# A pre-LN linear-attention and GeGLU block on one core: the opening loads reordered over two rings, two tiles only centred, and the rest of the layernorm taken in pairs

## The chip, the cores and the metric

The kernel runs on one core of a Trainium2 chip. The metric is device time in microseconds (us) of one execution; lower is better. Before the change the median of 16 runs is 194.26 us (193.64 to 194.85).

## The reference

x is 2048 tokens of 448 features in bf16. The block is an attention without softmax, with 16 heads of 28, and a gated feed-forward part of width 1792. Each is preceded by a layernorm without weights and followed by a residual.

```python
n   = layernorm(x)                      # mean and variance over the 448 features
q, k, v = heads(n @ wqkv)               # wqkv: 448 x 1344
pq, pk  = phi(q), phi(k)                # phi(t) = (t + 1 if t > 0 else exp(t)) + 1e-6
kv  = einsum("bhsd,bhse->bhde", pk, v); z = pk summed over the tokens
h   = x + ((pq @ kv) / (pq . z + 1e-6)) @ wo
m   = layernorm(h)
out = h + (gelu(m @ w_gate) * (m @ w_up)) @ w_down
```

kv and z are sums over all the tokens, so the attention's output cannot begin before the K part of every token is done.

## The kernel before

The tokens are 16 tiles of 128. Everything stays in SBUF. The stages, by what TensorE (PE) does:

1. **Loads and warm-up.** SyncE (SP) issues x tile 0, the Q and K weights (`dwqk`, the first 384 rows, and `dwqk_t`, the 64-row tail), then x tiles 2 to 15, the V weights and wo; ScalarE (ACT) issues x tile 1 (lines 303 to 313, all through `dma`, line 284). Meanwhile PE runs 40 matmuls of 128 columns on a tile of ones (L342), whose result is not used.
2. **Layernorm 1 and projections** (`ln_tile`, `k_tile`, `q_tile`). Statistics are made on VectorE (DVE): `bnst` (L348) and `bnag` (L349). rstd is exp(-0.5 ln(var + eps)), two ACT instructions per tile: `ln` (L355), `rstd` (L357). Tiles 0 to 3 are normalized on DVE (`normD`, L370), transposed by PE in two halves (`tr0`, `tr1`, L378) and copied from PSUM by ACT (`evxA`, L383) and DVE (`evxD`, L385). Tiles 4 to 15 are normalized on GpSimd (POOL; `negm` L352, `normP` L388) and transposed by DMA from SP's queue (`xT`, L390). `k_t` and `q_t` are four accumulating matmuls each (L404). The first two read the half that ACT copied, the last two the half that DVE copied, and the fourth the weight tail. For K: `ek` (ACT exp, L415), `ck` (DVE, L416), `pk` (DVE, from PSUM, L417), then `pt_t`, four matmuls that add the normalized tile against pk (L423). For Q: `eq` and `rq` (ACT exp and relu, L431, L432).
3. **kv and w2** (L462, L471): the small matrices that join v, the heads and wo.
4. **Attention output and layernorm 2** (`a2_pair`), by pairs of tiles: `cq`, `aq` (DVE), `t1` (POOL), `dr`, `rd`, `pn` (DVE), a transpose (`tro` on PE for the first pair, `oT` by DMA for the others, L510), `out2` (PE, L523), `hr` (DVE residual), layernorm 2, and a transpose into hnT (`trh` on PE for tiles 0 and 1; `nhP` on POOL, `wrap` on DVE, `hT` by DMA, L561, for the others). w_down is loaded by one DMA, `dwd`, 1568 KB, from SP's queue.
5. **Feed-forward** by chunks of 2, 2, 4, 4, 4 tiles: `gu` (PE, L603 and L605), `ge` (ACT gelu, L623), `hm` (DVE product, L625), `down` (PE, L575), `fo` (DVE residual), `do` (output DMA).

No engine chooses its order at run time. Every piece of work is a task, numbered in the order in which the source adds it, with semaphores for its data. The five strings of `ORDERS` list the numbers of the tasks of PE, ACT, DVE, POOL and SP in the order in which that engine runs them; a waiting task holds up all that is behind it on its engine.

Of the kernel before, what the change touches and what calls it, by code (L numbers as in the profile page):

```python
# [5 lines left out]
BF16 = mybir.dt.bfloat16  # L6
F32 = mybir.dt.float32
ALU = mybir.AluOpType
# [7 lines left out]
    "26 32 34 43 63 41 66 71 76 52 59 50 61 79 84 70 87 75 99 83 116 111 91 126 103 138 115 150 162 130 174 142 154"  # L16
    " 187 200 213 219 166 229 178 191 245 204 235 217 233 179 249 192 205 218 234 250 254 251 291 257 295 299 293"
    " 260 315 297 266 319 317 263 320 269 278 275 356 333 337 272 434 439 387 444 449 454 459 418 464 506 511 516"
    " 469 526 521 490 472 531 536 578 583 588 562 541 544 593 598 603 608 613 618 623 628 633 638 643 675 648 651"
    " 706 654 657 722 727 732 737 742 747 752 757 762 767 772 777 782 787 804 809 814 819 824 829 795 792 801 798"  # L20
    " 834 839 844 849 854 859 864 869 874 877 880 883 886",
    "3 25 29 30 38 39 33 42 64 47 56 48 57 65 67 72 94 51 95 78 60 106 107 80 77 121 122 86 133 88 85 134 145 146"
    " 100 157 169 158 170 112 118 182 183 195 196 127 139 117 208 209 240 224 241 151 163 225 175 188 201 214 220"
    " 221 230 246 236 237 285 308 288 289 256 253 255 252 312 258 347 351 259 294 316 298 268 318 267 261 265 264"
    " 379 383 262 327 328 270 280 329 330 279 277 271 334 276 273 274 339 435 437 442 414 440 410 445 447 452 450"
    " 457 455 462 460 467 465 482 509 507 486 514 519 512 517 527 529 558 554 524 522 532 534 539 537 579 581 671"
    " 586 584 589 667 591 702 596 594 599 601 606 604 698 611 609 614 616 621 619 626 624 629 631 634 636 641 639"
    " 644 646 723 725 728 730 733 735 740 738 745 743 748 750 755 753 760 758 763 765 770 768 773 775 780 778 785"
    " 783 790 788 807 805 812 810 817 815 822 820 825 827 832 830 837 835 842 840 845 847 852 850 857 855 860 862"
    " 867 865 870 872",  # L30
    "27 28 36 37 31 40 35 44 45 54 46 55 92 49 93 58 104 68 105 73 53 69 62 119 74 120 131 81 132 143 82 144 89 167"
    " 155 90 156 168 101 180 206 102 181 193 113 194 114 222 207 238 128 239 223 129 140 141 340 152 153 164 165 303"
    " 176 341 177 342 304 189 301 190 202 215 302 343 216 203 231 232 372 247 248 373 374 375 286 305 287 307 290"
    " 309 311 310 346 292 350 296 300 352 313 348 314 353 349 321 382 322 378 323 324 405 325 380 331 326 381 332"
    " 335 384 336 385 406 338 357 360 358 403 359 404 361 413 362 438 409 436 443 415 411 441 412 416 475 446 448"
    " 476 367 391 453 451 388 370 392 458 477 547 456 693 463 478 481 461 389 393 390 422 468 466 548 549 485 510"
    " 508 423 487 483 488 484 419 520 518 424 515 550 401 420 513 662 421 398 660 557 528 553 691 429 523 530 555"
    " 663 432 525 694 661 559 470 560 494 491 533 535 556 540 538 692 580 582 670 495 587 473 585 666 590 566 701"
    " 668 496 567 592 563 672 669 564 492 673 565 703 493 704 545 568 597 595 600 602 697 607 605 542 612 610 699"
    " 700 615 617 622 620 627 625 630 632 635 637 640 501 676 647 645 679 504 677 576 649 680 573 681 652 678 710"  # L40
    " 711 642 707 655 708 709 658 712 724 726 729 731 720 717 734 736 741 739 689 746 744 686 749 751 756 754 761"
    " 759 764 766 771 769 774 776 781 779 786 784 791 789 808 806 813 811 818 816 823 821 826 828 833 831 796 793"
    " 799 802 838 836 843 841 846 848 853 851 858 856 861 863 866 868 873 871 875 878 881 884 887",
    "15 13 0 14 1 19 20 21 17 18 16 96 22 97 108 109 123 124 24 135 147 136 148 23 159 171 160 172 184 185 197 198"
    " 242 226 210 211 227 243 306 344 345 376 377 408 407 364 363 365 366 479 369 480 551 395 394 396 397 400 552"
    " 426 425 427 428 431 664 665 696 695 498 497 499 500 569 570 571 575 503 572 682 683 684 685 688 714 713 715"
    " 716 719",
    "2 4 5 6 7 8 9 10 11 12 98 110 125 137 149 161 173 186 199 212 228 244 281 282 283 284 354 386 417 368 371 355"
    " 489 402 399 430 433 471 561 674 474 705 546 502 577 505 574 543 656 721 718 650 653 659 690 687 797 794 803"
    " 800 879 876 885 882 888",  # L50
# [120 lines left out]
def bass_sequential_preLN__linear_attn_block__glu_gated_geglu__prompt_kernel(  # L171
# [11 lines left out]
    N_PE_TR = 4  # L183
    B1_CHUNKS = [2, 2, 4, 4, 4]
    WARM = 40
    T1_DVE = (0,)
    SEQ = "Q0 K0 K1 Q1 K2 Q2 K3 K4 K5 Q3 K6 K7 K8 K9 K10 K11 K12 K13 Q4 K14 Q5 K15 Q6 Q7 Q8 Q9 Q10 Q11 Q12 Q13 Q14 Q15"
# [3 lines left out]
    with es:  # L191
# [6 lines left out]
        xnn = sb("xnn", [128, XN_R, 512], BF16)  # L198
        xnT = sb("xnT", [128, T, 4, 128], BF16)
# [17 lines left out]
        rs1 = sb("rs1", [128, T], F32)  # L217
        st2 = sb("st2", [128, T, 6], F32)
# [29 lines left out]
        b_x = bufs("x", T)  # L248
        b_xn = bufs("xn", XN_R)
        b_xnT = [bufs("xnT%d_" % t, 2) for t in range(T)]  # L250
        b_ones2 = _Buf("ones2")
        b_wqk, b_wv = bufs("wqk", 2), bufs("wv", 2)
# [3 lines left out]
        b_epsd = _Buf("epsd")  # L256
# [34 lines left out]
        def dma_w3(q, dst, c0, c1, b, name):  # L291
            return dma(q, dst[:, 0:3, :], A_wqkv[0:384, c0:c1].rearrange("(k p) n -> p k n", p=128), [b[0]], name)
# [8 lines left out]
        for dst, b, nm_ in ((wqk_sb, b_wqk, "wqkpad"), (wv_sb, b_wv, "wvpad")):  # L301
            op("pool", lambda e, dst=dst: e.memset(dst[:, 3, :], 0.0), [], [b[1]], nm_)
        dma_x("sp", 0, 1)
        tx1 = dma_x("act", 1, 2)
        dma_w3("sp", wqk_sb, 0, 2 * D, b_wqk, "dwqk")
        dma_w1("sp", wqk_sb, 0, 2 * D, b_wqk, "dwqk_t")
        dma_x("sp", 2, 4)
        dma_x("sp", 4, 8)
# [4 lines left out]
        two = dma("sp", wo_sb[:, :, :], A_wo.rearrange("(g p) n -> p g n", p=GW), [b_wo], "dwo")  # L313
# [13 lines left out]
           [b_mtmp], [b_mask], "mask_b")  # L327
        op("pool", lambda e: e.memset(pt_sb[:, 3, :], 0.0), [], [b_pt[3]], "ptpad")
        op("pool", lambda e: e.memset(pqn[:, :, :, :, GW:128], 0.0), [], [b for l in b_pqn for b in l], "pqnpad")

        tbl1 = G.add("act", lambda e: e.preload_act_table_set("natural_log_exp_and_others"), name="tbl1", kind="nosync", after=[tx1])
# [7 lines left out]
        def warm_fn(e):  # L339
            ins = None  # L340
            for _ in range(WARM):
                ins = e.matmul(ps[:, 3, 0:128], ones_bf[:], ones_bf[:], start=True, stop=True)  # L342
            return ins
        G.add("pe", warm_fn, r=[b_ones], w=[b_ps[3]], name="warm")
# [20 lines left out]
        def ln_tile(t):  # L365
            ln_stats(t, x_sb[:, t, :], b_x[t], st1, mv1, b_st1, b_mv1, "1")
            ln_rstd_act(t, t + 1, mv1, ln1, rs1, b_mv1, b_ln1, b_rs1, "1")
            i = t % XN_R
            if t < N_PE_TR:
                op("dve", lambda e: e.tensor_scalar(xnn[:, i, 0:D], x_sb[:, t, :], mv1[:, t, 0:1], rs1[:, t:t + 1], ALU.subtract, ALU.mult),  # L370
                   [b_x[t], b_mv1[t], b_rs1[t]], [b_xn[i]], "normD_%d" % t)
                for h, (eng, k0, k1) in enumerate((("act", 0, 2), ("dve", 2, 4))):
                    bk = BK_TR[t % 2][h]

                    def ftr(e, k0=k0, k1=k1, bk=bk):
                        ins = None
                        for k in range(k0, k1):
                            ins = e.transpose(psb[:, bk, (k - k0) * 128:(k - k0 + 1) * 128], xnn[:, i, k * 128:(k + 1) * 128], ident[:])  # L378
                        return ins
                    G.add("pe", ftr, r=[b_xn[i], b_ones2, b_ident], w=[b_ps[bk]], name="tr%d_%d" % (h, t))  # L380
# [5 lines left out]
            else:  # L386
                ln_negm(t, t + 1, mv1, nm1, b_mv1, b_nm1, "1")
                op("pool", lambda e: e.tensor_scalar(xnn[:, i, 0:D], x_sb[:, t, :], nm1[:, t:t + 1], rs1[:, t:t + 1], ALU.add, ALU.mult),  # L388
                   [b_x[t], b_nm1[t], b_rs1[t]], [b_xn[i]], "normP_%d" % t)
                G.add("sp", lambda e: e.dma_start_transpose(xnT[:, t, :, :], xnn[:, i, :]), r=[b_xn[i], b_ones2], w=b_xnT[t], name="xT_%d" % t, kind="dma", after=[two])  # L390
# [16 lines left out]
        def proj_reads(t):  # L407
            return [(b_xnT[t][0], 0), (b_xnT[t][1], 2), (b_wqk[0], 0), (b_wqk[1], 3)]
# [19 lines left out]
        def q_tile(t):  # L428
            bk = slot()
            G.add("pe", lambda e, W: proj(e, W, t, bk, 0), r=proj_reads(t), w=[b_ps[bk]], name="q_%d" % t, mw=True)  # L430
            act_exp(lambda e: e.activation(eq[:, t, :], ps[:, bk, 0:D], AF.Exp), [b_ps[bk]], [b_eq[t]], "eq_%d" % t)  # L431
            act_exp(lambda e: e.activation(pq[:, t, :], ps[:, bk, 0:D], AF.Relu), [b_ps[bk]], [b_pq[t]], "rq_%d" % t)  # L432
# [258 lines left out]
```

## Time and profile before

| what | value |
|---|---|
| median of 16 runs | 194.26 us |
| the profiled execution: its time / its span | 194.31 us / 192.5 us |
| TensorE clock granted in the span | 1.0 of full speed |
| PE's stretch from the first transpose to the last matmul | 5.37 to 190.1 us |
| one projection, `pt` or `out` matmul of 448 columns, back to back | 0.189 us, four in 0.756 us |
| DVE busy from 12.02 to 18.24 us / from 50.11 to 73.42 us | 6.22 of 6.22 / 22.16 of 23.31 us |

The page gives the busy time of each engine; the timeline lists instructions in order of time; the view of waits says what an engine waited for. PE loads weights (PEld) ahead of the matmuls that use them, and matmuls overlap, so a stall may appear as a wait of PEld while PE still counts as busy. The gap between starts in the timeline, against 0.189 us for a matmul of 448 columns, is then the measure.

### The profile page before, as it was taken

What the parts mean: (1) busy time and instruction counts of PE and PEld (TensorE: products, weight loads), DVE (VectorE), ACT (ScalarE), POOL (GpSimd) and SP (SyncE); (2) the same over time, 40 slices, a digit from 0 to 9 for tenths busy, and PEclk for the clock granted to TensorE, in tenths of its full rate; (3) what the DMA queues carried; (4) which work ended last, traced back from release to release, by engine and by line L of the source; (5) the groups of instructions that cost most, each with busy time, mean ns of one, the idle gap of its engine ahead of it and who ended that gap; (6) DMA issues with size and microseconds to landing.
All of it is one profiled execution on the core that took longest, in us unless ns stands there. A gap on an engine that the chain in (4) does not pass through costs nothing.

```text
span 192.5 us, 4152 instructions
## 1 busy us (share of the span) xinstructions
PE 187.3 (97%) x1572; PEld 108.2 (56%) x1572; DVE 131.6 (68%) x355; ACT 77.9 (40%) x226; POOL 50.8 (26%) x92
## 2 busy tenths in 40 slices
PE   7989999999999899999999999999999999999994
PEld 7544455554778677564445655545556655445454
DVE  2899988999999988979957446736544442244412
ACT  3697736599954242043044420024444430044200
POOL 7068620560263387404190000450000000000000
PEclk9999999999999999999999999999999999999999
DMA  6976458998206967520032124305600001010011
GB/s 198 377 187 80 95 109 174 223 219 113 58 0 121 171 215 134 123 47 7 3 78 40 44 49 93 90 8 121 145 0 3 0 3 44 6 48 3 0 48 48
DMA packets 35331, 16.97 MB, mean 88 GB/s; under 512 B 27696, under 2 KB 34032, under 8 KB 35312
## 3 DMA queue, kind: packets, MB, share of 16 engines
q1 hardware_dynamic: 35168, 16.60, 38.4%
q8 instruction: 12, 0.20, 0.4%
q10 hardware_dynamic: 144, 0.11, 0.2%
q14 instruction: 7, 0.06, 0.1%
HBM read 8.26 MB, written 1.84 MB: 52 GB/s over the span
## 4 chain that ended last, share of the span: by engine, by line
PE 77%; DMA 5%; DVE 3%; ACT 2%; issue 0%; SPq 0%; DVEq 0%; POOL 0%
PE ps L603 34%; PE ps L575 22%; PE ps L404 6%; PE ps L523 5%; PE ps L605 5%; DMA wd_sb<-in_B_w_down_dram 4%; PE ps L423 4%; DMA xnT<-xnn 2%; DVE hh L625 1%; ACT eq L431 1%; DVE x_sb L529 1%; PE ps L471 0%; ACT pq L432 0%; PE ps L462 0%; PE ps L550 0%
## 5 line engine op out<-in xcount | busy, mean ns | idle before, releaser
L603 PE MATMUL ps<-hnT,wgu_sb 64*128 64x512 bf16 (+1 forms) x490 | 86.4, 334 | 0.5 <-ACT gl L623 0.5
L605 PE MATMUL ps<-hnT,wgu_sb 64*128 64x512 bf16 (+1 forms) x490 | 86.6, 334 | 0.0
L623 ACT ACTIVATE gl<-ps 128x256 bf16<-128x256 f32 x112 | 37.1, 380 | 84.2 <-PE ps L605 82.2
L625 DVE TENSOR_TENSOR hh<-ps,gl 128x256 bf16<-128x256 f32 x112 | 42.9, 418 | 31.3 <-ACT gl L623 31.1
L603 PEld LDWEIGHTS ps<-hnT,wgu_sb 64*128 64x128 bf16 x490 | 45.3, 94 | 28.8 <-issue 3.0
L605 PEld LDWEIGHTS ps<-hnT,wgu_sb 64*128 64x128 bf16 x490 | 42.7, 94 | 4.7 <-DVE hh L625 1.7
L575 PE MATMUL ps<-wd_sb,hh 128*128 128x448 bf16 (+1 forms) x238 | 43.6, 342 | 0.1
L575 PEld LDWEIGHTS ps<-wd_sb,hh 128*128 128x128 bf16 x238 | 23.0, 98 | 20.1 <-issue 0.8
L404 PE MATMUL ps<-wqk_sb,xnT 128*128 128x448 bf16 x128 | 27.6, 353 | 0.6 <-ACT xnT L383 0.5
L488 POOL TENSOR_TENSOR t<-pq,zbc 128x448 f32<-128x448 bf16 x15 | 16.6, 1115 | 39.3 <-DVE pq L484 22.2
L579 DVE TENSOR_TENSOR x_sb<-ps,x_sb 128x448 bf16<-128x448 f32 (+1 forms) x17 | 10.0, 592 | 18.2 <-PE ps L575 18.2
L348 DVE BATCH_NORM_STATS2 st<-x_sb 128x6 f32<-128x448 bf16 x32 | 19.2, 611 | 3.4 <-DMA x_sb<-in_A_x_dram 3.4
L404 PEld LDWEIGHTS ps<-wqk_sb,xnT 128*128 128x128 bf16 x128 | 12.0, 98 | 11.8 <-DMA xnT<-xnn 1.0
L423 PE MATMUL ps<-pk,xnn 128*128 128x448 bf16 x64 | 14.1, 353 | 0.0
L523 PE MATMUL ps<-w,pqnT 112*128 112x448 bf16 x64 | 13.6, 353 | 0.2 <-DVE hn L541 0.2
L529 DVE TENSOR_TENSOR x_sb<-ps,x_sb 128x448 bf16<-128x448 f32 x16 | 9.6, 613 | 2.7 <-PE ps L523 2.7
L558 POOL TENSOR_SCALAR hn<-x_sb,nm,rs 128x448 bf16<-128x448 bf16 x14 | 10.8, 777 | 0.8 <-POOL rs L361 0.2
L415 ACT ACTIVATE e<-ps 128x448 bf16<-128x448 f32 x16 | 8.5, 539 | 5.6 <-PE ps L404 5.5
L352 POOL TENSOR_SCALAR nm<-mv 128x1 f32<-128x1 f32 (+1 forms) x19 | 4.0, 218 | 24.9 <-DVE mv L349 24.3
L495 DVE TENSOR_TENSOR pqn<-pq,rd 128x448 bf16<-128x448 bf16 x16 | 10.0, 642 | 0.0
L417 DVE SCALAR_TENSOR_TENSOR pk<-ps,e 128x448 bf16<-128x448 f32 x16 | 9.7, 615 | 0.2
L491 DVE TENSOR_REDUCE den<-t 128x16 f32<-128x448 f32 x16 | 9.7, 604 | 0.0
(65 smaller groups left out, 125.3 us busy)
## 6 DMA issues: line engine op xcount, KB each, us to landing
out_dram<-x_sb SPq DMA_DIRECT2D x15, 112.0 KB, 1.8
wd_sb<-in_B_w_down_dram SPq DMA_DIRECT2D x1, 1568.0 KB, 7.0
x_sb<-in_A_x_dram SPq DMA_DIRECT2D x3, 448.0 KB, 5.3
wgu_sb<-in_B_w_gate_dram SPq DMA_DIRECT2D x1, 896.0 KB, 12.0
wgu_sb<-in_B_w_up_dram SPq DMA_DIRECT2D x1, 896.0 KB, 16.4
wqk_sb<-in_A_wqkv_dram SPq DMA_DIRECT2D x1, 672.0 KB, 4.4
wgu_sb<-in_B_w_gate_dram SPq DMA_DIRECT2D x1, 672.0 KB, 5.9
wgu_sb<-in_B_w_up_dram SPq DMA_DIRECT2D x1, 672.0 KB, 8.4
```

The lines of the kernel that those rows point to most:

```text
L348: op("dve", lambda e: e.bn_stats(st[:, t, :], src_ap), [b_src], [b_st[t]], "bnst%s_%d" % (tag, t))
L404: ins = e.matmul(ps[:, bk, 0:D], xnT[:, t, k, :], wqk_sb[:, k, c0:c0 + D], start=(k == 0), stop=(k == 3))
L423: ins = e.matmul(ps[:, BK_PT[c], 0:D], xnn[:, t % XN_R, c * 128:(c + 1) * 128], pk[:, ip, :], start=(t == 0), stop=(t == T - 1))
L488: op(eng, lambda e, t=t, n=n: e.tensor_tensor(t1[:, n, :], pq[:, t, :], zbc[:, :], ALU.mult), [b_pq[t]] + b_z, [b_t1[n]], "t1%s_%d" % (eng ...
L523: ins = e.matmul(ps[:, BK_OUT[n], 0:D], pqnT[0:GW, i2, n, g, :], w2[:, g, :], start=(g == 0), stop=(g == NG - 1))
L529: op("dve", lambda e, t=t, bo=bo: e.tensor_tensor(x_sb[:, t, :], ps[:, bo, 0:D], x_sb[:, t, :], ALU.add), [b_ps[bo], b_x[t]], [b_x[t]], "h ...
L558: op("pool", lambda e, t=t, sh=sh: e.tensor_scalar(hn[:, sh, 0:D], x_sb[:, t, :], nm2[:, t:t + 1], rs2[:, t:t + 1], ALU.add, ALU.mult), [b ...
L575: ins = e.matmul(psO, hh[:, j, (t % HR) * 128:(t % HR + 1) * 128], wd_sb[:, j, c0:c1], start=(j == 0), stop=(j == NJ - 1))
L603: e.matmul(psG[:, jj * N:(jj + 1) * N], wgu_sb[A_, k, j * 128:(j + 1) * 128], hnT[A_, ka_, c0:c0 + N], start=(k == 0), stop=(k == NK - 1))
L605: ins = e.matmul(psU[:, jj * N:(jj + 1) * N], wgu_sb[B_, k, j * 128:(j + 1) * 128], hnT[B_, kb_, c0:c0 + N], start=(k == 0), stop=(k == NK ...
L623: G.add("act", lambda e, gi=gi, cs_=cs_, psG=psG: e.activation(gl[:, gi, cs_], psG[:, cs_], AF.Gelu_apprx_tanh), r=[b_ps[BK_G[i]]], w=[b_g ...
L625: op("dve", lambda e, dst=dst, srcU=srcU, srcL=srcL: e.tensor_tensor(dst, srcU, srcL, ALU.mult), [b_ps[BK_U[i]], b_glh], [b_ar[j_][t % HR] ...
```

## The change

The opening loads: K's and Q's weights become two loads of 336 KB. SP issues K's weights first, then x2, Q's weights, x3, x4 to 5, x6 to 7 and the rest as before. ACT issues x0, x1 and the weight tail. The zero padding of the weight tiles moves from POOL to DVE and covers only the 64 rows that the tails don't fill.

```diff
-        for dst, b, nm_ in ((wqk_sb, b_wqk, "wqkpad"), (wv_sb, b_wv, "wvpad")):
-            op("pool", lambda e, dst=dst: e.memset(dst[:, 3, :], 0.0), [], [b[1]], nm_)
-        dma_x("sp", 0, 1)
-        tx1 = dma_x("act", 1, 2)
-        dma_w3("sp", wqk_sb, 0, 2 * D, b_wqk, "dwqk")
-        dma_w1("sp", wqk_sb, 0, 2 * D, b_wqk, "dwqk_t")
-        dma_x("sp", 2, 4)
-        dma_x("sp", 4, 8)
+        for dst, b, nm_ in ((wqk_sb, b_wqp, "wqkpad"), (wv_sb, b_wvp, "wvpad")):
+            op("dve", lambda e, dst=dst: e.memset(dst[B_, 3, :], 0.0), [], [b], nm_)
...
+        dma_x("act", 0, 1)
+        dma_x("act", 1, 2)
+        dma_w1("act", wqk_sb, 0, 2 * D, [None, b_wqt], "dwqk_t")
+        dma_wqk(1)
+        dma_x("sp", 2, 3)
+        dma_wqk(0)
+        dma_x("sp", 3, 4)
+        dma_x("sp", 4, 6)
+        dma_x("sp", 6, 8)
         dma_x("sp", 8, 12)
         dma_x("sp", 12, 16)
```

Tiles 0 and 1 go to the transposes centred but not scaled: `cen` takes the place of `normD`. rstd is applied later as the scale of the activations that read the projections (`ek`, `eq`, `rq`, and a new `rk`, a relu, for K), and POOL makes the normalized tile (`normP_0`, `normP_1`) that `pt` needs. For tile 1 the statistics are made on ACT (`asum_1`, `asq_1`, each an activation with a sum over the row) and POOL (`msq_1`).

```diff
+            elif t in ACT_ST:
+                act_exp(lambda e: e.activation(e1[:, 2, :], x_sb[:, t, :], AF.Identity, scale=1.0 / D, accum_out=mv1[:, t, 0:1]),
+                        [b_x[t]], [b_e1[2], b_mv1[t]], "asum_%d" % t)
+                act_exp(lambda e: e.activation(e1[:, 3, :], x_sb[:, t, :], AF.Square, scale=D ** -0.5, accum_out=mv1[:, t, 1:2]),
+                        [b_x[t]], [b_e1[3], b_msq], "asq_%d" % t)
...
+                if t in CEN:
+                    src_t, b_src, b_pad = xc[:, t % 2, :], b_xc[t % 2], b_xcp
+                    op("dve", lambda e: e.tensor_scalar(xc[:, t % 2, 0:D], x_sb[:, t, :], mv1[:, t, 0:1], None, ALU.subtract), [b_x[t], b_mv1[t]], [b_xc[t % 2]], "cen_%d" % t)
...
+            if t in CEN:
+                act_exp(lambda e: e.activation(pk[:, ip, :], psK, AF.Relu, scale=sc), [b_ps[bk]] + rsc, [b_pk[ip]], "rk_%d" % t)
+                op("dve", lambda e: e.tensor_scalar(e1[:, i, :], e1[:, i, :], 1.0, EPS, ALU.min, ALU.add), [b_e1[i]], [b_e1[i]], "ck_%d" % t)
+                op("dve", lambda e: e.tensor_tensor(pk[:, ip, :], pk[:, ip, :], e1[:, i, :], ALU.add), [b_pk[ip], b_e1[i]], [b_pk[ip]], "pka_%d" % t)
```

From tile 4 on, `ln`, `rstd` and `negm` are formed for two tiles at once (`lnP`, `rstdP`, `negmP`), after the statistics of both. WARM goes from 40 to 36.

```diff
-    WARM = 40
+    LN_PAIR = 4
+    CEN = (0, 1)
+    ACT_ST = (1,)
+    WARM, WARM2, NW2 = 36, 0, 0
...
-    SEQ = "Q0 K0 K1 Q1 K2 Q2 K3 K4 K5 Q3 K6 ...
+    SEQ = "K0 K1 Q0 K2 Q1 K3 Q2 Q3 K4 K5 K6 ...
```

All five strings of `ORDERS` are new. With the numbers replaced by the tasks' names, the parts that the prediction uses are:

```
PE   before: warm tr0_0 tr1_0 tr1_1 q_0 tr0_1 k_0 k_1 q_1 tr1_2 tr0_3 tr0_2 tr1_3 k_2 q_2 pt4_0 k_3 pt4_1 k_4
PE   after:  warm tr0_0 tr1_0 tr1_1 tr0_1 k_0 q_0 k_1 q_1 tr1_2 tr0_2 tr1_3 tr0_3 k_2 q_2 k_3 pt4_0 pt4_1 k_4
ACT  after:  dx0 dx1 dwqk_t tbl1 asum_1 ln_0 asq_1 evxA_0 rstd_0 ln_1 rstd_1 evxA_1 ek_0 ln_2 rk_0 rstd_2 rq_0 ln_3 rstd_3 lnP_4 evxA_2
DVE  before: bnst_0 bnag_0 bnst_1 bnag_1 normD_0 normD_1 evxD_0 evxD_1 bnst_2 bnst_3 bnag_2 bnag_3 bnst_4 normD_2 bnag_4 normD_3
             bnst_5 ck_0 bnag_5 ck_1 evxD_2
DVE  after:  wqkpad bnst_0 bnag_0 cen_0 cen_1 wvpad evxD_0 bnst_2 evxD_1 bnag_2 bnst_3 bnst_5 bnst_4 normD_2 bnag_4 bnag_3 ck_0
             bnag_5 bnst_6 normD_3 bnst_8 evxD_2
DVE  before, layernorm 2: hr_0 dr_5 bnst2_0 dr_4 bnag2_0 hr_1 ... nhD_0
DVE  after,  layernorm 2: hr_0 pn_2 bnst2_0 cq_8 hr_1 bnag2_0 ... nhD_0
PE   before: gu2_0 gu2_1 out2_4 gu2_2 .. gu2_5 out2_6 gu2_6 gu2_7 gu2_8 gu2_9 down_0
PE   after:  gu2_0 gu2_1 out2_4 gu2_2 .. gu2_5 out2_6 gu2_6 gu2_7 gu2_8 down_1 gu2_9
SP   before: oT_1 oT_2 oT_3 hT_2 hT_3 dwd oT_4
SP   after:  oT_1 oT_2 dwd oT_3 hT_2 hT_3 oT_4
POOL before: ... nhP_2 t1_8 nhP_3 ...      after: ... t1_8 ... nhP_2 nhP_3 ...
DVE  after, feed-forward: hm_4 cq_11 bnst2_5 hm1_5 rd_8 hm0_5 aq_11 hr_7 hr_6 cq_10 bnst2_7 hm0_6 cq_15 hm1_6
```

## Prediction before the run

> **What bounds the kernel now.** First the page's busy line.
>
> ```profile
> PE 187.3 (97%) x1572; PEld 108.2 (56%) x1572; DVE 131.6 (68%) x355; ACT 77.9 (40%) x226; POOL 50.8 (26%) x92
> ```
>
> PE bounds it, and the change leaves PE its matmuls, all but four for warming. So it can give only stalls back. To find them I read the opening's timeline against 0.189 us for a matmul of 448 columns.
>
> ```profile
> 1.07 4.29 PE L342 MATMUL ps<-ones_bf 128*128 128x128 bf16 x40 [1.07 <-POOL ones_bf L315]
> ...
> 5.37 0.38 PE L378 MATMUL ps<-ident,xnn 128*128 128x128 bf16 x4
> ...
> 6.06 0.29 PE L378 MATMUL ps<-ident,xnn 128*128 128x128 bf16 x2 [0.32 <-DVE xnn L370]
> ...
> 6.20 0.92 PE L404 MATMUL ps<-wqk_sb,xnT 128*128 128x448 bf16 x4
> ...
> 10.49 1.69 PE L404 MATMUL ps<-wqk_sb,xnT 128*128 128x448 bf16 x8 [0.51 <-ACT xnT L383]
> ...
> 12.02 0.92 PE L423 MATMUL ps<-pk,xnn 128*128 128x448 bf16 x4
> ```
>
> From 5.37 to 12.02 PE does 16 transposes (0.055 each by the later rows) and 24 projection matmuls: 0.88 + 4.54 = 5.4 us of work in 6.65, so 1.25 us is lost. From there on the view of waits, for weight loads:
>
> ```profile
> PEld ps L603 <- issue: 3.0, 7, 0.8
> ...
> PEld ps L404 <- DMA xnT<-xnn: 1.0, 2, 0.5
> ...
> PEld ps L575 <- DMA wd_sb<-in_B_w_down_dram: 0.4, 1, 0.4
> ```
>
> The starts around these waits give the true losses. Between 12.02 and 38.2 us, 0.17 and 0.25 us are lost to `xT` transposes (at 18.24 and 23.80). The longest "issue" wait, 0.8, is the start of gu2_7: its pair of matmuls comes at 65.72, after one at 64.95, a loss of 0.66. Its cause is in SP's line for `hT` at 61 us:
>
> ```profile
> L561 SPq DMA_TRANSPOSE hnT<-hn x1: 2478/2478/2478, 61.0 to 61.0; - x1
> ...
> DMA to landing us min/median/max: 4.6/4.6/4.6
> ```
>
> hT_3 lands at 60.99 + 4.6 = 65.6, where other `hT` take 2.9. Then down_0 waits for w_down, as the chain shows:
>
> ```profile
> 63.52 7.04 DMA wd_sb<-in_B_w_down_dram
> 70.61 2.82 PE ps L575 x14
> ```
>
> The last gu2_9 pair began at 70.21, so this costs 70.61 - 70.32 = 0.29. From 50.83 to 73.36 PE does 20.9 us of work in 22.5: 1.65 lost.
>
> **The opening.** Landings go by bytes: in the trace x2 to 3 landed at 6.54 after 1232 KB, x4 to 7 at 7.7 after 1680 KB, so 390 KB/us. With the new order K's weights, x0, x1 and the tail (672 KB) are there at 5.1, x2 (784) at 5.4, Q's weights (1120) at 6.25, x3 (1232) at 6.5, x4 to 5 (1456) at 7.1. x0 was 2.6 us under way (2.7 from ACT's ring); I keep 3.4 for it, and 4.3 for x1, now second on its ring (issue 0.40). SP issues 11 loads instead of 10 at 0.39 to 0.58 each, done some 0.5 us later; its next task, xT_4, ran at 11.37, so this costs nothing. ACT issues three loads (0.40 each) before its table load of 1.28, which then ends at 3.3, ahead of x1.
>
> The trace's 36 warm matmuls end at 1.04 + 36 x 0.107 = 4.9 (`ones` is now POOL's first). DVE: bnst_0 3.4, bnag_0 4.1, cen_0 4.3 to 4.7 (0.37, as normD; ln and rstd no longer lie before it). `ident` and the new padding `xcpad` stand early on POOL, where the larger paddings of 0.85 and 0.47 have gone. So transposes start at 4.95, not 5.37. ACT: asum_1 4.3; an activation with a row sum is not in the trace. Below: 0.43, the spacing of 448-column activations; above: 1.08, twice one's 0.54. I take 0.55, its nearest row. Then ln_0, asq_1 4.9 and only behind it evxA_0, 5.35 to 5.75. cen_1 waits for asum_1 until 5.0; behind it on DVE stand wvpad (0 to 0.47, POOL's row for the double size; I take 0.2) and evxD_0, done at 5.8. So k_0 starts at 5.8, where q_0 started at 6.20: 0.4 us.
>
> Then DVE is the limit. With spacings read off the dense rows (bnst 0.54, bnag 0.09, normD 0.30, ck 0.17, evxD 0.20): bnst_2 5.7, evxD_1 6.2, bnst_3 6.55 (x3), bnst_5 7.2 (x5), bnst_4 7.75, normD_2 8.3, then bnag_4, bnag_3, ck_0, bnag_5 and bnst_6 before normD_3, 9.6 (before: 9.05); bnst_8 9.9, evxD_2 10.45 to 10.75 (before: 10.29). PE's order puts tr1_3 and tr0_3, which need normD_3, ahead of k_2; so k_2 starts at 10.25, stops at its third matmul until 10.75, and q_2 ends at 11.9 against 12.02. **-0.1 us**; bounds -0.4 (k_0's gain kept) and +0.7 (each row sum at 1.08).
>
> **Up to kv.** The pairs save ACT six `ln` and `rstd` (6 x 0.49) and POOL six `negm` (6 x 0.21), none of them on PE's path; the even tile waits for one more bnst and bnag (0.7). POOL gets normP_0 and normP_1 (0.71 each), hidden behind evxD_2: pt4_0 is due at 12.6. DVE loses bnst_1, bnag_1 and two `pk` from PSUM (0.61) for two `pka` (0.38 as `aq`); ACT gets two `rk` (0.53), hidden while PE projects. By the same walk normP_4 starts at 10.1, not 10.63; xT_6, _8, _10 and _12 land 0.5 to 1 us ahead of their `k`. Both waits go; pk_4, at the end of a DVE that was busy 6.22 of 6.22 us, is late by some 0.15. **-0.25 us**; -0.42 to +0.5 (one `xT` late by a POOL slot of 0.71 less the 0.2 of cover).
>
> **kv to feed-forward.** dr_5 and dr_4 (0.52 each) leave the path from hr_0 to nhD_0, one pn_2 (0.54) enters it, hr_1 comes before bnag2_0: some 0.5 us sooner. PE waited there 0.17 for nhD_0's consumers and 0.13 before gu2_0, which after evh_1 stays DVE-bound. **-0.15 us**; -0.4 to +0.3.
>
> **Feed-forward's start.** dwd moves ahead of oT_3, hT_2 and hT_3 on SP. oT_2 was issued at 49.82, so w_down goes at 51.05 and, at its 7.0 us, lands at 58.1; from 54 to 58 us the DMA engines moved nothing. oT_3, issued at 57.28 before, may wait 0.8 us behind it; out2_6 is due at 61.9 and it lands in 3.0, cover 1.6. So 0.29 goes, although down_1 comes one `gu` earlier. nhP_3 no longer stands behind t1_8, wrap_3 stays near 60.6 on DVE, and at the usual 2.9 hT_3 lands at 63.6, before gu2_7 (65): 0.66 goes. That the slow 4.6 was an accident of that transfer is an assumption; if it stays, so does the 0.66. Late next is hm_6: after hm_5 come aq_11, hr_7, hr_6, cq_10, bnst2_7 (0.3 + 0.54 + 0.54 + 0.19 + 0.54) before its first half, so gu2_8 waits 0.3 to 0.5. Sum **-0.6 us**; -0.95 to +0.5 (hT_3 unchanged, hm_6 late). The rest keeps its work and its tail of 2.4 us.
>
> **Sum.** -0.1 - 0.25 - 0.15 - 0.6 = -1.1. The profiled execution took 194.31, 0.05 above the median: 193.2 us.
>
> [...] Warm matmuls fell from 314 to 219 ns among those started from 4.8 to 5.1, 3.95 us after the first; until then one took 107 ns. With 36 the same moment, 5.0, falls among the transposes. I take it to come at that time, whatever PE runs. [...]
>
> **Rivals.**
> 1. *DVE only hands the stalls on.* The opening gives nothing (evxD_2 is the last to arrive there, and each row sum above 0.55 delays it), and where hT_3 and w_down no longer stall PE, hm_6 and its successors do. DVE's 22.16 busy of 23.31 us speak for it; against it, that half of that stage's loss has a transfer at its end, not DVE. With the opening and layernorm 2 at 0 and half of the other two terms: 194.31 - 0.4 = 193.9, up to 194.6. Chance 0.18.
> 2. *w_down holds up the transposes (slower).* oT_3, hT_2 and hT_3 now stand behind 1568 KB on one queue. For it: the page shows a load of 896 KB on this queue that took 16.4 us to land. Against it: that one was queued behind others and beside transposes, and w_down itself took 7.0. The point is oT_3: with its 1.6 of cover, w_down may take 7.0 + 0.8 + 1.6 = 9.4 us; each us beyond is a us for out2_6 and all behind it. At 11 us it costs 1.6: 194.31 - 1.1 + 1.6 = 194.8; at 13, 196.8. Chance 0.12.
> 3. *The clock comes late.* At the rate of the warm matmuls, 107 ns for 128 columns where the later rows have 55, the 16 projection matmuls of tiles 0 and 1 take 16 x 0.189 = 3.0 us more: 194.31 - 1.1 + 3.0 = 196.2. Chance 0.06.
>
> My forecast, 192.5 to 193.85, has 0.58; a further 0.06, where the opening keeps its 0.4 and hm_6 is not late, lies below it. The range 192.5 to 194.9 leaves out that and the upper part of rivals 2 and 3. A measurement of this kernel can tell about 0.2% (0.4 us) from no change: faster 0.64, same 0.16, slower 0.20.
>
> **What would show it.** Right: first projection at 5.8; k_2 near 10.3 with a wait for L385's half inside; w_down landed before 60 and no wait for it; hT_3 at 2.9. Wrong: asum_1 over 0.75 us; projection matmuls at 0.38 us after 5.3; oT_3 or hT landing behind w_down; waits for `xT` that grow.

## The result and the profile after

The change made the kernel slower. The median of 9 runs is 195.9 us (195.06 to 198.01); before, on the same chip, 194.13 us (48 runs, 193.46 to 194.92). The ratio is 1.0081, 95% interval 1.0062 to 1.01. Four single executions whose granted clock fell to 0.991 over the span (one of after, two of f3 and one of h2 below) are left out of the ratios, though not of the medians; the last section shows what goes with such a fall.

The profiled execution took 195.43 us, its span 193.6 (before: 194.31 and 192.5), so the two profiles explain 1.12 of the 1.77 us between the medians. The busy line first:

```profile
PE 187.7 (97%) x1568; PEld 109.9 (57%) x1568; DVE 132.1 (68%) x355; ACT 77.9 (40%) x220; POOL 51.6 (27%) x90
```

PE does the same work less four warm matmuls, so the loss is again in stalls. The timeline of after, TensorE only (start, duration, then the idle time before it and what ended it in brackets):

```profile
5.05 0.59 PE L421 MATMUL ps<-ident,xc 128*128 128x128 bf16 x4
6.00 0.61 PE L421 MATMUL ps<-ident,xc 128*128 128x128 bf16 x4 [0.37 <-DVE xc L410]
6.65 3.28 PE L449 MATMUL ps<-wqk_sb,xnT 128*128 128x448 bf16 x16
...
10.88 0.40 PE L421 MATMUL ps<-ident,xnn 128*128 128x128 bf16 x4 [0.72 <-DVE xnn L413]
11.11 2.59 PE L449 MATMUL ps<-wqk_sb,xnT 128*128 128x448 bf16 x12
13.53 1.68 PE L475 MATMUL ps<-pk,xnn 128*128 128x448 bf16 x8
...
22.35 0.92 PE L449 MATMUL ps<-wqk_sb,xnT 128*128 128x448 bf16 x4 [1.09 <-DMA xnT<-xnn]
```

The first transposes come 0.3 us earlier than before, the first projection 0.45 us later, and at 22.35 k_7 waits 1.09 us for xT_7, longer than any wait for an `xT` before. At 13.53 seven projections are done; before had done the same work (six and one `pt`) at 12.02 + 0.756 = 12.78. By points of equal work, before and after:

| stretch | before | after | difference | predicted |
|---|---|---|---|---|
| start to seven projections | 12.78 | 13.53 | +0.75 | -0.1 |
| from there to kv | 38.19 - 12.78 = 25.41 | 39.75 - 13.53 = 26.22 | +0.81 | -0.25 |
| kv to gu2_0 | 50.83 - 38.19 = 12.64 | 52.45 - 39.75 = 12.70 | +0.06 | -0.15 |
| gu2_0 to the first two chunks' end | 73.36 - 50.83 = 22.53 | 74.19 - 52.45 = 21.74 | -0.79 | -0.6 |
| from there to the second chunk of four | 125.94 - 73.36 = 52.58 | 127.22 - 74.19 = 53.03 | +0.45 | 0 |
| to the end of the span | 66.56 | 66.38 | -0.18 | 0 |

The gain of the feed-forward's start is there. No wait for w_down is left; it was issued at 53.17 and took 8.0 us. hT_3, issued at 62.5, took 3.1 us where it had taken 4.6. What comes after it gives part back: in the view of waits (us in total, times, longest) the wait for `hm` before `gu`, 1.7 us in 10 parts before, is now

```profile
PEld ps L665 <- DVE hh L685: 4.9, 24, 0.3
```

Of it, 1.9 us lie between 74.19 and 127.22, where before had 0.5 (between 73.36 and 125.94). These are waits for loading weights: they grew by 1.4 us, and PE lost 0.45 us in that stretch, by the table.

### The profile page after: what moved, and what is told of

It is laid out like the page before. It is cut to its first block, busy times and chain, and to the rows that moved or that the text cites. A ratio compares the mean times of both kernels' runs of the same rounds, so it can differ in the third digit from the quotient of the medians.

```text
span 193.6 us, 4137 instructions
## 1 busy us (share of the span) xinstructions
PE 187.7 (97%) x1568; PEld 109.9 (57%) x1568; DVE 132.1 (68%) x355; ACT 77.9 (40%) x220; POOL 51.6 (27%) x90
## 4 chain that ended last, share of the span: by engine, by line
PE 84%; DVE 3%; DMA 2%; POOL 1%; issue 0%; DVEq 0%; POOLq 0%
PE ps L663 29%; PE ps L635 22%; PE ps L665 15%; PE ps L449 6%; PE ps L583 6%; PE ps L475 4%; DMA xnT<-xnn 2%; POOL xnn L432 1%; DVE pqn L555 1%; PE ps L531 0%; PE ps L522 0%; DVE hn L601 0%; DVE x_sb L589 0%; POOL nm L369 0%; DVE st L365 0%
## 5 line engine op out<-in xcount | busy, mean ns | idle before, releaser
L639 DVE TENSOR_TENSOR x_sb<-ps,x_sb 128x448 bf16<-128x448 f32 (+1 forms) x17 | 10.1, 594 | 20.3 <-PE ps L635 20.3
L365 DVE BATCH_NORM_STATS2 st<-x_sb 128x6 f32<-128x448 bf16 x31 | 18.3, 613 | 2.4 <-DMA x_sb<-in_A_x_dram 2.3
L432 POOL TENSOR_SCALAR xnn<-x_sb,nm,rs 128x448 bf16<-128x448 bf16 x14 | 9.9, 714 | 5.6 <-PE ps L475 2.8
L462 ACT ACTIVATE e<-ps 128x448 bf16<-128x448 f32 x14 | 7.3, 550 | 8.4 <-PE ps L449 6.0
L555 DVE TENSOR_TENSOR pqn<-pq,rd 128x448 bf16<-128x448 bf16 x16 | 10.6, 662 | 0.0
L475 PEld LDWEIGHTS ps<-pk,xnn 128*128 128x128 bf16 x64 | 6.2, 98 | 5.9 <-DVE pk L469 0.2
```

Of the source, the lines that this page charges most:

```text
L365: op("dve", lambda e: e.bn_stats(st[:, t, :], src_ap), [b_src], [b_st[t]], "bnst%s_%d" % (tag, t))
L475: ins = e.matmul(ps[:, BK_PT[c], 0:D], xnn[:, t % XN_R, c * 128:(c + 1) * 128], pk[:, ip, :], start=(t == 0), stop=(t == T - 1))
L555: op("dve", lambda e, t=t, n=n, i=i, i2=i2: e.tensor_tensor(pqn[:, i2, n, :, 0:GW].rearrange("p g (h d) -> p g h d", h=4), pq[:, t, :].rea ...
```

## The experiments

Each was timed against before on the same chip (a run's ratio and interval; its median beside it). "Head" is the order up to kv, "tail" that from kv on.

### The two halves

`e1_old_head_new_tail` is before with the tail's part of the five ORDERS strings taken from after; `e2_new_head_old_tail` is after with before's tail.

> The kernel before up to the last projection that kv needs, and from kv on the changed kernel's order on all five engines (w_down issued after oT_2, nhP_3 next to nhP_2, layernorm 2 without dr_4 and dr_5 in its path). Theory: the change's loss lies ahead of kv (PE was 1.56 us later at kv) and its new order behind kv gives about 0.8 back, so this runs faster than before by 0.5 to 0.9 us, near 193.4. Rival (the stalls at hT_3 and w_down were accidents of one execution, or the gain behind kv was only slack of a later start): no change, 194.1. Rival (the new order behind kv is itself worse, the 0.3 lost after 73 us shows it): slower by 0.3 or more.

> The changed kernel up to the last projection before kv, and from kv on the order of the kernel before. Theory: the whole loss of the opening and of the K part shows, 1.5 us or more over before, 195.6 to 196.5, no better than the changed kernel. Rival (the new order behind kv causes the loss): near before, 194.1 to 194.5.

Measured: the old head with the new tail 1.0058 (1.0037 to 1.008), 195.21; the new head with the old tail 1.0108 (1.0073 to 1.0143), 195.9. So the head alone carries the whole loss, but the new tail behind the old head was no gain either. In its profile kv came at 37.68 and gu2_0 at 50.38, 0.45 us earlier than before, and out2_4 then waited for oT_2:

```profile
54.87 0.35 PE L523 MATMUL ps<-w,pqnT 112*128 112x448 bf16 x1 [1.26 <-DMA pqnT<-pqn]
```

oT_2 had taken 4.9 us to land instead of 3.0.

### The opening

```diff
e3:  -        dma_x("act", 0, 1)          +        dma_x("sp", 0, 1)
e4:  -    ACT_ST = (1,)                   +    ACT_ST = ()        # bnst_1, bnag_1 on DVE ahead of cen_1
f2 (in before):  -    WARM = 40           +    WARM = 36
f3:  + 4 warm matmuls behind tr1_0, 2 behind tr0_1
```

> The changed kernel with one load moved: x0 is issued by SP ahead of K's weights, as in the kernel before, so that x1 is the first on ACT's ring. Theory (the order on the rings): x1 lands near 3.6 instead of 4.8 us, the first row sum starts a us earlier, k_0 starts at 5.8 instead of 6.65, and 0.4 to 0.8 us of the loss goes; about 195.2. Rival (the length of the chain on ACT and DVE is what counts, not x1): k_0 moves by less than 0.3 and the time by less than 0.2.

> The changed kernel with the statistics of tile 1 made on DVE (bnst, bnag) as in the kernel before, not by two row sums on ACT and one instruction on POOL; loads unchanged. If the row sums on ACT are what delays the opening: evxA_0 starts at 5.4 instead of 6.15, k_0 by 0.3 to 0.5 earlier, and up to 0.5 us of the loss goes. If x1's late landing (4.8) is: cen_1 stays at 5.6, k_0 at 6.4 or later, and DVE, with one bnst more, hands all of it on: within 0.2 of the changed kernel.

> The kernel before with 36 warm matmuls instead of 40. In the five profiles so far the matmuls became fast at times between 4.1 and 10 us; in the one at 10 us (changed kernel with tile 1 on DVE) projections ran at 0.37 instead of 0.19 us each. Theory (fewer warm matmuls and longer gaps let the release slip in some executions): single times up to 3 us above the rest appear, and the median is 0.1 to 0.6 above before. Rival (four warm matmuls don't matter; the first transposes wait for normD anyway): same as before within 0.1, no outliers.

> The changed kernel with six more warm matmuls, in the gaps that PE has between the transposes and k_0 (four after tile 0's transposes, two after tile 1's); nothing else waits for them. Theory (the clock's late release makes the changed kernel's high single times and part of its median): the times above 196.2 go and the median falls by 0.3 to 0.6, to about 195.4. Rival (the high times come from elsewhere, transposes by DMA above all): spread and median as the changed kernel's, 195.9.

Measured: x0 on SP 1.008 (1.0047 to 1.0114), 195.54; statistics on DVE 1.0094 (1.0066 to 1.0121), 195.81; before with 36 warm matmuls 1.0031 (1.001 to 1.0052), 194.55; after with filling matmuls 1.0138 (1.0107 to 1.0168), 198.06. None of these undoes the loss. With the filling no execution was faster than 196.4. Before with 36 warm matmuls lost some 0.6 us by its ratio, without the high single times that the theory asked for: in its profile kv is only 0.13 later, and oT_1 took 4.8 us instead of 4.0. So fewer warm matmuls alone can cost that much.

With x0 on SP, x1 lands at 3.4 and the first projection starts at 5.54. But seven projections are done at 13.11, only 0.42 earlier than in after. q_0 waits for Q's weights until 6.83, DVE waits 0.49 us for x2 and 0.30 for x3 (landed at 7.09), and normD_3 again comes late:

```profile
5.54 0.92 PE L450 MATMUL ps<-wqk_sb,xnT 128*128 128x448 bf16 x4 [0.23 <-ACT rs L375]
6.83 2.44 PE L450 MATMUL ps<-wqk_sb,xnT 128*128 128x448 bf16 x12 [0.38 <-DMA wqk_sb<-in_A_wqkv_dram]
...
10.44 0.40 PE L422 MATMUL ps<-ident,xnn 128*128 128x128 bf16 x4 [0.82 <-DVE xnn L414]
```

With tile 1's statistics on DVE (e4), evxA_0 runs at 5.45 instead of 6.15, and still the first projection starts at 6.60, against 6.65 in after (cen_1 runs 0.2 later than in after, behind bnst_1 on DVE). So the row sums on ACT are at most a small part of what makes k_0 late. What e4 shares with after, and e3 doesn't, is x1's landing at 4.8 to 4.9.

### The pairs

`f4_new_no_pairs` and `g1_new_no_pairs_b` are after with one rstd for each tile; they differ in where ACT's order puts them. `g3_old_pairs` is before with the pairs alone.

```diff
f4, g1:  -    LN_PAIR = 4      +    LN_PAIR = 16
f4  ACT: evxA_3 ln_6 rstd_6 ln_8 rstd_8 rq_1 eq_1 ek_2 ln_7 rstd_7 ek_3 ln_9 rstd_9
g1  ACT: evxA_3 ln_6 rstd_6 rq_1 eq_1 ek_2 ek_3 ln_8 rstd_8 ln_7 rstd_7 ln_9 rstd_9
```

> The changed kernel with ln, rstd and negm of tiles 4 to 15 formed tile by tile again (bnag_6 moved ahead of bnag_8, each normP behind its own negm). Theory (the pairs delay normP_6 and leave SP's queue of transposes idle from 14.4 to 15.9 us, so that k_7 waits 1.09): xT_6 is issued by 14.5, k_7 waits less than 0.3, and 0.6 to 1.0 us go, to about 195.0. Rival (k_7 waited because its transpose took 3.5 instead of 2.5 us, which comes and goes): the wait stays or moves to another tile, and the time changes by less than 0.3.

> The kernel after with one rstd for every tile again, as in the run before it, but with ScalarE's order mended: of the singles only tile 6's stand ahead of k_2's and k_3's exponentials, tiles 8, 7 and 9 behind them, so that pk_2 is not late and q_3 does not wait for K2's PSUM bank. Theory (the pairs cost the K part its 0.8 us, because the even tile's rstd waits for the odd tile's statistics and SyncE's transposes then have no slack): no wait over 0.4 us for xT or pk between 13.5 us and kv, kv at 38.9 to 39.2 (after: 39.75), the time 0.5 to 0.9 under after's 195.9, so 195.0 to 195.4, and no single time above 197. Rival (the K part loses by DVE, whose order has more work ahead of pk and which has to catch up whatever the pairs do): kv stays at 39.6 or later and the time within 0.3 of 195.9.

> The kernel before with the pairs alone: one ln, rstd and negm for tiles 4 and 5, 6 and 7 and so on, everything else and the orders as they were. If the pairs by themselves cost the K part 0.8 us: xT_6 is issued 0.6 to 0.8 later than 14.0, the waits for xT between 12 and 38 us grow from 0.4 to about 1, kv at 38.6 to 39.0 (before: 38.19), the time 0.4 to 0.8 over before. If pairs cost only together with after's opening (projections 0.8 later on PE, six statistics ahead of normD_3): kv within 0.2 of 38.2 and the time within 0.3 of before.

Measured: f4 1.0111 (1.0082 to 1.0139), 195.83; g1 1.0051 (1.003 to 1.0071), 195.09; g3 1.0034 (1.0012 to 1.0056), 195.19. In f4 the waits for `xT` are gone, but q_3 waits 1.08 us for pk_2, which those early singles delay: its order is at fault. In g1 PE loses only some 0.3 us from 14 to 39 us (25.25 us for 132 matmuls of 0.189). g3 loses 0.7 us against before by its ratio (0.2 to 1.1), 0.9 by the medians: the pairs seem to cost something by themselves, though in its profile oT_2 was late too (4.8 us).

### The tail, and a sum

`f1_old_early_wd` is before with `dwd` moved ahead of oT_3; `g4_old_head_wd_late` is the first run with `dwd` back behind hT_3; `g2_sum` is after without pairs (as g1), with x0 on SP and before's tail.

> The kernel before with one task moved: w_down's load is issued right after oT_2, ahead of oT_3, hT_2 and hT_3. In the mixed kernel (old opening, new order behind kv) out2_4 waited 1.3 us for oT_2, which took 4.9 us with w_down issued 1.3 us behind it. Theory (w_down's bytes hold up oT_2): out2_4 starts 0.5 to 1.3 us late here too and the time is 0.2 to 0.9 above before, 194.5 to 195.1. Rival (that late transpose was one execution's accident, like hT_3 in the kernel before): the wait for w_down (0.29) and hT_3's (0.66) go, 0.3 to 0.9 faster, near 193.6.

> Before's order up to kv and after's order from kv on, as in the first run, but with w_down's load back behind hT_3 on SyncE. Theory (in the first run the tail lost because oT_2 landed late beside w_down, 4.9 us): oT_2 lands in 3.0 to 3.5, out2_4 at 53.0 to 53.6 instead of 54.9, the wait for w_down of 0.3 to 0.5 is back, and the time is 194.3 or less, level with before or up to 0.3 faster. Rival (the tail's new order of DVE and ScalarE loses by waits for hm in the feed-forward, 0.45 us between 74 and 126 us in the first run's profile, and more in other executions): the time stays at 194.9 to 195.4.

> After with three parts undone together: no pairs (with the mended order of ScalarE), x0 issued by SyncE first of all, and before's order from kv on. What is left of the change is tiles 0 and 1 only centred, tile 1's sums on ScalarE, and K's weights ahead of Q's. Theory (opening by the ring order, K part by the pairs, each on its own): the first projection at 5.5 to 5.8, kv at 38.2 to 38.5 as in before (38.19), the time 194.1 to 194.5. Rival (the centring with its row-sum activations, scaled activations and order of DVE loses by itself): kv at 39.0 or later, the time 195.0 or more.

Measured: f1 1.001 (0.9989 to 1.003), 194.41, no difference; g4 1.0183 (1.0129 to 1.0237), 198.48; g2 1.0038 (1.0015 to 1.0062), 195.01. g2 came out at the rival's numbers (kv at 39.13), but two of its `xT` took 4.5 and 3.9 us, so it doesn't decide. g4 met neither expectation: oT_2 took 4.8 us again, with nothing behind it, so w_down was not what delayed it. And since the new tail asks for w_down at 69.1, a late load now stalls PE for 2.13 us, after which its granted clock reads 0.50. The windows of g4 (each with its length, the busy us and the instructions of PE, PEld, DVE, ACT and POOL, then the granted clock, the DMA share and GB/s):

```profile
70.00:72.00 2.00, 0.77 (x5) 0.41 (x6) 2.00 (x8) 0.00 (x0) 0.97 (x1) 1.00 0.03 5
72.00:74.00 2.00, 2.00 (x7) 0.86 (x6) 1.46 (x7) 0.00 (x0) 1.37 (x4) 0.50 0.03 8
74.00:76.00 2.00, 2.00 (x12) 0.75 (x11) 0.00 (x0) 0.00 (x0) 0.52 (x1) 0.65 0.00 0
```

### What makes a transpose late

oT_2 was late in two programs at the same place. The DMA view has a queue that the kernel doesn't issue to, named "instruction" (q8, packets of 16 KB; q14, 8 KB). Around the issue of before's xT_6 (14.0 us), from 14.9 to 15.1 us, it shows one packet and the landing (45.0% of 16 engines over 0.2 us is 1.44 us of one engine, the packet's whole time):

```profile
q8 instruction: 1, 0.02, 45.0%
...
xnT<-xnn SPq DMA_TRANSPOSE x1, 4.2
```

The 20 profiles of this study have 660 transposes. Take 2.5 us as the usual landing for `xT` and 3.0 for `oT` and `hT`. Of the 452 with no such packet starting between issue and usual landing, 1 landed 1 us late or more, and 16 others 0.5 us or more; 8 of these 16 went directly behind a late one, and 5 were oT_3 beside w_down. Of the 60 with a packet of q8 starting 0.5 to 2 us after the issue, 50 landed 1 us late or more. Where the packets fall differs from program to program. There is one profile of each program, so whether the packets fall alike in its other executions is not shown. The next runs move them: fewer warm matmuls of more columns, at the same pace the same time on PE (4.02 us for 36 of 128 columns in after and for 9 of 512 in i2), nothing else changed. If the packets make the transposes late, a packet that moves hits other transposes than before.

```diff
h1, h3, i1:  WARM 40 -> 20      h2, h4:  WARM 36 -> 18      (256 columns each)
-  ins = e.matmul(ps[:, 3, 0:128], ones_bf[:], ones_bf[:], start=True, stop=True)
+  ins = e.matmul(ps[:, 3, 0:256].rearrange("p (a b) -> p a b", a=2), ones_bf[:],
+                 ones_bf[:, :].unsqueeze(1).to_broadcast([128, 2, 128]), start=True, stop=True)
i2:  WARM 36 -> 9, 512 columns each, in the same way
```

h1 is before, h2 after, h3 the first run (e1), h4 and i2 the run g1, i1 the run g3.

> The kernel before with 20 warm matmuls of 256 columns in place of 40 of 128: the same time on TensorE, 40 instructions fewer on its queue. [...] The time within 0.5 of before, in either direction, by which transposes it hits. Rival (late landings come from the transposes' own neighbours on their queue): xT_6, oT_1 and hT_3 are late as in before, wherever the packets are.

> The kernel after with 18 warm matmuls of 256 columns in place of 36 of 128, 36 instructions of TensorE fewer. [...] The time between 194.9 and 196.4, by where the packets fall. Rival: the wait for xT_7 is there as before, 0.9 to 1.2, and the time 195.9 within 0.3.

> The first run (before's order up to kv, after's from kv on) with 20 warm matmuls of 256 columns. There oT_2 took 4.9 us with w_down behind it, and 4.8 with w_down 14 us later; both had a packet of q8 at 52.5. Theory: the packet moves, oT_2 lands in 3.0 to 3.3, out2_4 starts at 53.2 to 53.7 instead of 54.87, and the time is 194.3 or less (195.21 in the first run). Rival: oT_2 is late by itself, again 4.5 to 5.0, and the time 195.0 to 195.4.

> After with one rstd for every tile and the mended order of ScalarE (195.09), with 18 warm matmuls of 256 columns. If the opening is what is left of the loss, the time stays between 194.7 and 195.3 whatever the packets do, with the first projection at 6.6; if the packets on xT_6 and xT_9 (4.3 and 3.5 in that run) are what is left, kv comes at 38.5 and the time at 194.4 or less.

> Before with the pairs alone (195.19 with 40 warm matmuls) and 20 warm matmuls of 256 columns, so that the packets of the instruction queue fall elsewhere. If the pairs cost before 0.9 us by themselves, the time is again 0.5 to 1.0 over before's. If the 0.9 was mostly where a packet fell (oT_2 4.8 us, xT_6 3.6 in that run), the time is within 0.5 of before's, as that of before with the same 20 wide matmuls (194.79).

> After with one rstd for every tile and the mended order, with 9 warm matmuls of 512 columns: a third place of the packets for this order (195.09 with 36 warm matmuls, 195.83 with 18 wide ones). If taking out the pairs gives about 0.8 us, the three runs average 195.1 to 195.2, so this one gives 194.3 to 195.1. If the pairs are worth nothing beside the packets, they average as after and its wide form do, 195.8 to 195.9, and this one gives 195.5 to 196.6.

The ratios are the ones to compare, since the medians come from several chips, on which before itself had medians of 193.85 to 194.3:

| order | narrow warm matmuls | wide ones |
|---|---|---|
| before | 1 (194.3) | h1: 1.0029 (1.0009 to 1.0048), 194.79 |
| after | 1.0081 (1.0062 to 1.01), 195.9 | h2: 1.0088 (1.0053 to 1.0122), 195.82 |
| old head, new tail | e1: 1.0058 (1.0037 to 1.008), 195.21 | h3: 1.001 (0.9993 to 1.0027), 194.55 |
| after without pairs | g1: 1.0051 (1.003 to 1.0071), 195.09 | h4: 1.0068 (1.0046 to 1.009), 195.83; i2: 1.0071 (1.004 to 1.0102), 195.82 |
| before with pairs | g3: 1.0034 (1.0012 to 1.0056), 195.19 | i1: 1.0075 (1.0046 to 1.0104), 195.62 |

The packets moved, and the late transposes with them. In h1 the first q8 packet comes at 17.0 instead of 15.1 us; xT_6 lands in 2.5 us, and xT_7, issued at 15.85, in 3.7. In h3 the packet at 52.7 has gone to 56.3, and oT_2, issued at 51.29, is on time. The DMA view of e1 from 49.75 us, and of h3 from 51.25 us:

```profile
pqnT<-pqn SPq DMA_TRANSPOSE x1, 4.9
```

```profile
pqnT<-pqn SPq DMA_TRANSPOSE x1, 3.2
```

From gu2_0 to out2_4 takes 55.02 - 51.85 = 3.17 us in h3, as in after (55.61 - 52.45 = 3.16), and 4.49 in e1. That is the rival's end: oT_2 was not late by itself. The time is 194.55, not the 194.3 of the theory: in h3's profile kv comes at 39.15, 1.47 later than in e1's, where two `xT` beside packets took 3.6 and 3.7 us. And hT_3 of h1 is still late (4.6, with a packet at 61.8): not every packet moved, so what sets their places stays open. h4 and i2 were to show whether the pairs matter, and there a packet at 19.2 and 19.0 us strikes again: 195.83 is neither of h4's two cases, and i2's 195.82 fits its second, while the average of the three runs, 195.6, fits neither. In i2:

```profile
22.93 0.92 PE L451 MATMUL ps<-wqk_sb,xnT 128*128 128x448 bf16 x4 [1.01 <-ACT rs L376]
```

The releaser named, rstd, was done long before. The transpose issued at 17.9 took 4.9 us and landed at 22.8: that is the wait.

Of a transpose's delay beside a packet PE paid 1.26 us in e1, where oT_2 took 4.9 us instead of 3.0, and 1.01 in i2, where this one took 4.9 instead of 2.5.

## Why the prediction was wrong

I predicted 193.2 us, range 192.5 to 194.9, and gave slower a chance of 0.20. Two terms were off by 0.8 us or more, both in sign too, and both are in the head.

**The opening (-0.1; measured +0.75).** The failed step is the walk to k_0: x1's landing, on which too much stands. ACT's and DVE's lines of after, between 3.6 and 6.6 us:

```profile
4.83 0.58 ACT L394 ACTIVATE e<-x_sb 128x448 bf16<-128x448 bf16 x1 [1.25 <-DMA x_sb<-in_A_x_dram]
5.31 0.19 ACT L394 ACTIVATION_READ_ACCUMULATOR e<-x_sb 128x1 f32 x1
5.40 0.28 ACT L372 ACTIVATE ln<-mv,eps_t 128x1 f32<-128x1 f32 x1
5.59 0.56 ACT L396 ACTIVATE e<-x_sb 128x448 bf16<-128x448 bf16 x1
6.05 0.19 ACT L396 ACTIVATION_READ_ACCUMULATOR e<-x_sb 128x1 f32 x1
6.15 0.36 ACT L426 ACTIVATE xnT<-ps 128x256 bf16<-128x256 bf16 x1
```

```profile
3.69 0.63 DVE L365 BATCH_NORM_STATS2 st<-x_sb 128x6 f32<-128x448 bf16 x1 [2.31 <-DMA x_sb<-in_A_x_dram]
...
5.61 0.34 DVE L410 TENSOR_SCALAR xc<-x_sb,mv 128x448 bf16<-128x448 bf16 x1 [0.70 <-ACT e L394]
```

x0 landed 0.3 later than assumed and x1 at 4.8, not 4.3: "landings go by bytes" didn't hold for the second load of a ring. Nor did it for what came behind: the weight tail, third on ACT's ring, landed at 7.08 instead of 5.1, Q's weights at 7.27 instead of 6.25, and x3 at 7.47 instead of 6.5, with the same 1232 KB that had landed at 6.53 before. Why is open; from 2 to 3 us the DMA engines moved 153 GB/s, in before 251.

The first row sum was priced well (0.57 from asum_1 to ln_0, taken as 0.55; each has a second instruction of 0.19 that reads the sum out). Two ways lead from x1 to k_0. On ACT evxA_0 stands behind both row sums, at 6.15 instead of 5.35: 0.53 of it is x1's landing, 0.14 ln_0 (asq_1 followed it after 0.19, not 0.05) and 0.11 the second row sum. On DVE and PE, cen_1 (5.61 instead of 5.0) and tile 1's transposes (6.00) stand ahead of k_0 in the orders. So k_0 is at 6.65 instead of 5.8. In e4 the first way is free and the second still holds k_0 until 6.60; in e3, with x1 at 3.4 and the row sums as they are, it starts at 5.54. That shows x1's landing as the step that failed. Once it is mended the next late load shows: in e3 and g2 DVE waits for x3. The clock's release, as the change of the matmuls from 107 to 55 ns per 128 columns is called here, came at 6.5, not at 5.0 as assumed, and only slowed the transposes (0.107 us each instead of 0.055).

DVE then hands the delay on, as the prediction said it would: k_2 at 11.11, not 10.25. All seven profiles with x0 on ACT's ring and a clock released in time are late, 13.53 to 13.96 us at seven projections; nine with the old opening reach it at 12.61 to 13.02. Putting x0 on SP gives back 0.42 of it (e3, 13.11), and without the pairs 0.86 (g2, 13.10, against g1's 13.96). Without the pairs the point comes later still (13.79 to 13.96), probably because the singles put more instructions on ACT ahead of rk_1 and evxA_3: in g1 the last of the seven projections waits 0.27 us for evxA_3.

**Up to kv (-0.25; measured +0.81).** The prediction saw that the even tile waits for its neighbour's statistics (0.7 us), and checked only tile 4, where normP_4 then started at 10.96 instead of 10.1. It should have gone on to tile 6. That is the failed step here: the wait of the even tile's rstd, in ACT's order too. POOL's line in after (the first row is negmP_6, so tile 7's statistics were there at 13.0; the second is normP_6), then ACT's (ek_2 and ek_3, then lnP_6):

```profile
13.07 0.27 POOL L369 TENSOR_SCALAR nm<-mv 128x2 f32<-128x2 f32 x1 [0.66 <-DVE mv L366]
15.14 0.71 POOL L432 TENSOR_SCALAR xnn<-x_sb,nm,rs 128x448 bf16<-128x448 bf16 x1 [1.80 <-ACT rs L374]
```

```profile
13.61 1.02 ACT L462 ACTIVATE e<-ps 128x448 bf16<-128x448 f32 x2
14.46 0.35 ACT L372 ACTIVATE ln<-mv,eps_t 128x2 f32<-128x2 f32 x1
```

ACT reaches lnP_6 only at 14.46, behind rq_1, eq_1, ek_2 and ek_3. normP_6 started at 13.11 before, so xT_6 is issued at 15.88 instead of 14.0, with 1.5 us of idle queue ahead of it, and the cover of the later transposes is spent there. xT_7, issued at 18.71 with a q14 packet beside it, took 3.5 us, and 1.09 of that reached PE. From seven projections to kv all eight profiles with pairs take 25.89 us or more, of twelve without pairs seven take 25.41 or less. The other five take 26.0 to 26.4; in f4 this is pk_2, in the others a late `xT`. So the pairs remove cover, and the packets seem to decide what that costs. By the ratios they cost 0.7 and 1.5 us in before (g3, i1; of h1's 0.6 for moved packets the second may contain some). In after, taking them out gave 0.6 (g1 against after), 0.4 (h4 against h2) and 0.2 us (i2 against after), each within the intervals. What the pairs cost there on the average is not settled, nor how much of g1's gain is ACT's order, which has tile 6's rstd ahead of rq_1.

**kv to feed-forward (-0.15; +0.06).** The two `dr` did leave the path, but the stretch is no shorter: 12.70 in after, e1 and h3 alike. With the old tail it takes 12.50 to 13.41, by when oT_1 lands.

**Feed-forward's start (-0.6; -0.79) and what follows (0; +0.45).** hT_3 and w_down went as predicted, w_down with 8.0 us instead of 7.0. The predicted wait for hm_6 did not come there (0.2 us of waits for `hm` before 74.19). Behind it 0.45 us were lost; the waits for `hm` that grew there fit rival 1's mechanism, that they "become the stall", but no run tests it. The assumption that hT_3's 4.6 was an accident is wrong: in the seven other profiles with the old tail it takes 3.8 to 4.7, each time beside a packet at 61.7 to 63.2 us. In the new tail it is 3.1 in after, 3.2 to 4.0 in seven others, and 4.2 to 4.4 in h2, h3, h4 and i2. The tail as a whole gained -0.46 in after's profile. From kv to the span's end nine profiles with the new tail (g4 with its late w_down apart) take 153.8 to 154.1 us, the two whose oT_2 was late with w_down issued behind it (e1, f3) 155.2, and eight with the old tail 153.9 to 154.8. As a time no run shows the gain: e1 lost it by oT_2, and h3, whose kv came late, is level with before.

**Rivals.** None was what happened. w_down held nobody up: oT_3 beside it took 3.3 us instead of 3.0, within its cover. The late clock (rival 3) came in 2 of 11 profiles with the new opening, e4 and h2, in none of nine with the old. In e4:

```profile
6.20 0.60 PE L421 MATMUL ps<-ident,xc 128*128 128x128 bf16 x4 [0.58 <-DVE xc L410]
6.60 5.07 PE L449 MATMUL ps<-wqk_sb,xnT 128*128 128x448 bf16 x16
```

Sixteen projections take 5.07 us instead of 3.28 and seven are done at 15.07. With waits for `xT` of 2 us (f3, h2) this probably makes the upper end of the times, up to 198, and may be why the medians lie further apart than the two profiles.

No version ran faster than before: h3 (1.001) and f1 (1.001) are level with it.

## What to carry to other kernels

Walk the new order for every tile, not for the first: a part that saves instructions but makes one tile wait for another moves a queue's first issue, and all that stands behind it. When a kernel of 194 us is tuned to waits of 0.2 us, compare it in two or three versions that differ by a change that costs nothing, such as wider warm matmuls, which moves the packets: here that moved one and the same order by 0.1 to 0.9 us by the ratios, for two of the five orders (before, and e1 to h3) beyond the intervals. And price a stall of PE by its length too: behind the waits of 2.00 us (f3) and 2.13 us (g4) the granted clock read 0.50, which over some 3.4 us costs an estimated 1.7 us more; behind the 2.19 us of h2 it did not fall.

## What was not expected of the hardware

- **Packets of the instruction queue and transposes.** Told above: 50 of 60 landed 1 us late or more, against 1 of 452. In before the issue of hT_3 itself is stretched (2.48 us, most other `hT` 1.22); xT_6 and, in e1, oT_2 were issued in 1.27 and 1.23 and still landed late. By which path a packet delays a transpose is open.
- **When the matmuls become fast.** One matmul of 128 columns takes 107 ns at first and 55 later. The change comes at 5.1 us in before, 3.8 in e1, 5.7 in f2, 6.5 in after, 10.4 in e4 and 10.1 in h2, with the first matmul at 1.04 to 1.07 in each; in the other profiles it lies between 3.7 and 6.4. What sets the time is open. The granted clock doesn't show the release: in the view of windows it reads 1.00 from the start also in before, where the warm matmuls run at 107 ns. So go by the pace. The window from 8 to 10 us of e4 and of after, both with PE busy throughout, 7 matmuls against 14:

```profile
8.00:10.00 2.00, 2.00 (x7) 0.80 (x6) 1.31 (x4) 1.60 (x5) 0.80 (x2) 1.00 1.02 391
```

```profile
8.00:10.00 2.00, 2.00 (x14) 0.98 (x12) 2.00 (x9) 1.77 (x6) 1.48 (x3) 1.00 1.02 393
```

- **When the granted clock falls.** In f3 k_7 waited 2.00 us, and just behind the wait the granted clock fell to 0.50, for some 3.4 us:

```profile
22.00:24.00 2.00, 0.69 (x3) 0.37 (x4) 0.45 (x2) 0.14 (x1) 0.00 (x0) 0.87 0.84 126
24.00:26.00 2.00, 2.00 (x7) 0.78 (x6) 0.50 (x2) 0.64 (x2) 0.00 (x0) 0.50 0.39 80
26.00:28.00 2.00, 2.00 (x9) 0.88 (x8) 0.93 (x2) 0.00 (x0) 1.39 (x2) 0.78 0.26 51
```

  g4 did the same after 2.13 us, and four of its six runs have the granted clock of 0.991; h2, after 2.19 us, did not. So what decides whether it falls is not shown.
